# A list scheduler that keeps PSUM banks of the late attention reserved after their last reader

## The chip, the core and the metric

One core of a Trainium2 chip runs the whole program. The metric is device time in microseconds (us), median of the runs. The engines are TensorE (PE; its weight loads are listed as PEld), VectorE (DVE), ScalarE (ACT), GpSimd (POOL) and SyncE (SP), which issues most DMAs. Each engine takes its own instructions in the order in which they were written, and an instruction that waits holds up all behind it on that engine.

## What is computed

Windowed attention over 4 batch elements of 8 heads, 576 rows and 64 columns, and behind it two MLPs over the 2304 resulting rows of 512. Cut to what matters:

```python
scores = scale * np.matmul(q, k.transpose(0, 1, 3, 2))
masks = np.stack([mask_plain if h < H // 2 else mask_dil for h in range(H)], axis=0)
scores = np.where(masks[None, :, :, :], scores, -1000000000.0)
scores = scores - np.max(scores, axis=-1, keepdims=True)
attn = np.exp(scores)
attn = attn / (np.sum(attn, axis=-1, keepdims=True) + 1e-09)
x = np.matmul(attn, v)          # as (2304, 512) rows
h = x @ w_in1;  x = np.maximum(0.01 * h, h) @ w_out1
h = x @ w_in2;  out = (np.maximum(h, 0.0) + np.log1p(np.exp(-np.abs(h)))) @ w_out2
```

The arrays are float64 in the reference; the kernel converts the weights from their 8-byte form on the chip, and carries every product operand as two parts (a high and a low one), so that each logical product is three matmuls.

## The kernel before

**Stages.** The first MLP works on blocks of rows (`BLOCKS`: 256, 256, 352, then five of 288). For each block it walks 16 slices of the hidden layer: `g1` (line 715, 12 matmuls into bank `h`), an activation and a split on ACT (lines 731, 736) and DVE (line 740, `gl`), and two slots later `g2` (line 758, 12 matmuls into the four banks `yp`). The second MLP (`g3`, again line 715, and `g4`, line 854) begins after all blocks. Attention is cut into 8 windows of 288 rows with 4 pairs of heads each; window 0 and 1 are computed ahead of the first block ("early"), the windows 2 to 7 ("late") beside the MLP blocks before them: a window's result is the input of the block of the same number, so its last pair must be done when that block opens. I write "pair 6.3" for window 6, pair 3 (pairs 0 and 1 have the plain mask, 2 and 3 the dilated one).

**One late pair** is a chain over four engines: `trans_k`, `trans_q` (DVE, lines 510 and 517) - `scores` half 0 and half 1 (PE, line 562, each into a PSUM bank of tag `at`) - `mask` half 0 and 1 (DVE, line 576: adds the mask, PSUM bank to SBUF tile `s`) - `rowmax` (POOL, line 586) - `less_max` (DVE, line 590) - `exp` (ACT, line 593) - `pv_late` (PE, line 642, into an `at` bank) beside `sums` (POOL, line 650) - `spread` (DVE, line 658, needs both) - `recip` (DVE, lines 663 to 666) - `norm` (DVE, line 670, reads the `pv` bank) - `x_hi` (ACT, line 689) - `x_lo` (DVE, line 693, tile `xl`). There are only two `at` banks, one buffer `mx` for the two reductions of POOL (freed by `less_max`, then by `spread`) and two buffers of `s`.

**The same DVE** converts the weights: per piece a shift (268), a join (272), an add (281) and a split (311, tile `w`). The pieces of the first MLP are converted between the start and about 152 us, just ahead of their first use; those of the second are converted later, between the other work, and stored to DRAM.

**What sets the order.** No engine's order is written by hand. Each step is an `Op` with an engine, an assumed cost, `deps` (data), `acq` and `rel` (buffers it takes and frees) and a priority worked out backwards from due times. `run_schedule` walks time forward: when an engine is free it takes the ready operation of the least priority value whose buffers are free, and appends it to the result; the program is then emitted in that order. So the costs and delays in `Op` only set the order: on the chip, an instruction goes as soon as its engine, its inputs and its buffer are there. Three rules of the planner matter here. A buffer in `rel` is counted free the moment its reader ends:

```python
                _, _, o = heapq.heappop(finish)
                for r in o.rel:
                    free[r] += 1
```

An operation counts as ready a small delay (`lag`) after its inputs; PE operations of the late attention get `SLACK` on top (1.0 us before):

```python
            return late.get(a.eng, LATS if a.eng == b.eng else LAT) + b.slack
    ...
    NSPIN, LOCK, SLACK0, SLACK = 150, 1.2, 0.3, 1.0
```

And DVE operations marked `lock=True` are put back while a POOL reduction has just begun (`LOCK`, `WAIT`), since POOL and DVE get into each other's way there.

## Time and profile before

| | |
|---|---|
| median of 3 runs | 947.0 us (946.5 to 950.6) |
| the profiled execution | 947.08 us, of which the trace's span is 945.2 us |
| PE busy / weight loads | 907.5 us (96%) / 847.6 us (90%) |
| DVE busy | 728.5 us (77%) |
| ACT busy, POOL busy | 467.9 us (49%), 167.7 us (18%) |
| PE's granted clock, mean | 0.987 of full |

PE works nearly all the time, so what counts are the gaps that are left on it and the stretches at less than the full clock. The share of DVE hides that it is full in the stage in which the weights are converted and has room behind it. Up to about 60 us the early windows run; from 60 to about 475 us the first MLP with the late windows; behind that the rest of the first MLP and the second one, without attention.

### The profile page before, as it was taken

The numbers are of one execution on the slowest core, as the hardware profiler recorded it, in microseconds if no ns is written. First come the engines' busy times: TensorE is split into PE (matmuls) and PEld (weight loads), VectorE is DVE, ScalarE is ACT, GpSimd is POOL, SyncE is SP. The second block draws the span as 40 slices with busy tenths as digits, with TensorE's granted clock in tenths as the row PEclk, the third lists the DMA queues.
The fourth block names the chain that finished last, engine by engine and source line by source line (L and its number), as shares of the span: only waits on it lengthen the run. The fifth ranks groups of instructions, "written<-read, shape, count | busy, mean of one in ns | idle before, by whom it ended". The sixth has DMA issues, their size and how long they took to land.

```text
span 945.2 us, 15673 instructions
## 1 busy us (share of the span) xinstructions
PE 907.5 (96%) x5963; PEld 847.6 (90%) x5964; DVE 728.5 (77%) x1312; ACT 467.9 (49%) x935; POOL 167.7 (18%) x81
## 2 busy tenths in 40 slices
PE   6899988999999999899999999999999999999998
PEld 4789978999999999799999989989999899899996
DVE  3999998299696995977956787877877877877775
ACT  3768743334344353344447754544644645544544
POOL 5501233053251452423600000000000000000000
PEclk9979989999999999999999999999999999999999
DMA  8787113244445444433148700200200000000000
GB/s 225 213 245 254 20 27 54 70 116 128 126 109 140 102 126 121 123 106 124 54 152 266 243 27 1 68 1 1 68 1 1 34 1 0 34 1 1 34 1 34
DMA packets 139903, 81.51 MB, mean 86 GB/s; under 512 B 101172, under 2 KB 124724, under 8 KB 139828
## 3 DMA queue, kind: packets, MB, share of 16 engines
q1 hardware_dynamic: 137428, 79.92, 29.5%
q8 instruction: 47, 0.77, 0.3%
q10 hardware_dynamic: 2400, 0.59, 0.3%
q14 instruction: 28, 0.23, 0.1%
HBM read 62.65 MB, written 17.83 MB: 85 GB/s over the span
## 4 chain that ended last, share of the span: by engine, by line
PE 47%; DMA 1%; DVE 1%; ACT 1%; issue 0%; SPq 0%; DVEq 0%
PE h L715 23%; PE yo L854 21%; PE yp L758 3%; DMA raw<-in_moe_w_in_dram 1%; DMA w<-w 0%; DVE cf L272 0%; DMA y<-ys 0%; ACT hc L812 0%; ACT hc L811 0%; ACT w L308 0%; ACT ln L814 0%; DVE gl L841 0%; ACT gh L837 0%; DVE gl L740 0%; DVE cf L281 0%
## 5 line engine op out<-in xcount | busy, mean ns | idle before, releaser
L715 PE MATMUL h<-xh,w 128*128 128x384 f32 (+3 forms) x1792 | 446.2, 318 | 2.4 <-DVE w L311 2.2
L715 PEld LDWEIGHTS h<-xh,w 128*128 128x128 f32 x1792 | 315.4, 190 | 8.3 <-DVE w L311 3.3
L715 PE MATMUL h<-xl,w 128*128 128x384 f32 (+3 forms) x896 | 282.5, 315 | 0.3 <-DVE xl L693 0.3
L758 PE MATMUL yp<-gh,w 128*128 128x288 f32 (+2 forms) x1024 | 230.2, 300 | 0.7 <-DVE ys L768 0.7
L854 PE MATMUL yo<-w,gh 128*128 128x512 f32 x576 | 180.4, 394 | 1.4 <-ACT gh L837 1.4
L715 PEld LDWEIGHTS h<-xl,w 128*128 128x128 f32 x896 | 170.6, 190 | 4.8 <-DVE xl L693 0.5
L758 PEld LDWEIGHTS yp<-gh,w 128*128 128x128 f32 x1024 | 172.6, 189 | 1.8 <-DVE ys L768 1.0
L758 PE MATMUL yp<-gl,w 128*128 128x288 f32 (+2 forms) x512 | 151.7, 296 | 2.7 <-DVE gl L740 2.6
L811 ACT ACTIVATE hc<-h 128x384 f32<-128x384 f32 x96 | 47.1, 490 | 180.4 <-PE h L715 180.4
L854 PEld LDWEIGHTS yo<-w,gh 128*128 128x128 f32 x576 | 106.9, 188 | 19.6 <-ACT gh L837 2.6
L731 ACT ACTIVATE hc<-h 128x288 f32<-128x288 f32 (+2 forms) x128 | 52.0, 406 | 132.0 <-PE h L715 126.2
L854 PE MATMUL yo<-w,gl 128*128 128x512 f32 x288 | 114.4, 397 | 0.7 <-DVE gl L841 0.7
L650 POOL PARTITION_ALL_REDUCE sm<-s x24 | 92.8, 3866 | 59.7 <-ACT s L593 59.7
L740 DVE TENSOR_TENSOR gl<-hc,gh 128x288 fp32r<-128x288 f32 (+2 forms) x128 | 78.6, 616 | 31.9 <-ACT gh L736 31.0
L758 PEld LDWEIGHTS yp<-gl,w 128*128 128x128 f32 x512 | 96.9, 189 | 3.2 <-DVE gl L740 3.1
L822 DVE TENSOR_SCALAR z<-hc 128x384 f32<-128x384 f32 x96 | 34.5, 359 | 75.7 <-ACT hc L812 75.6
L586 POOL PARTITION_ALL_REDUCE mx<-s x24 | 49.5, 2061 | 224.1 <-DVE s L576 209.9
L854 PEld LDWEIGHTS yo<-w,gl 128*128 128x128 f32 x288 | 54.1, 188 | 14.1 <-DVE gl L841 1.7
L281 DVE CUSTOM_DVE_ANT_0 cf<-raw,cf 128x1024 uint16<-128x1024 uint16 (+1 forms) x48 | 62.2, 1295 | 1.5
L263 ACT ACTIVATE cf<-raw 128x512 f32<-128x512 f32 (+1 forms) x48 | 39.9, 831 | 42.4 <-DMA raw<-in_moe_w_in_dram 17.9
L736 ACT ACTIVATE gh<-hc 128x288 fp32r<-128x288 f32 (+2 forms) x128 | 56.7, 443 | 3.3
L841 DVE TENSOR_TENSOR gl<-ln,gh 128x384 fp32r<-128x384 f32 x96 | 53.5, 558 | 3.3 <-ACT gh L837 1.4
(83 smaller groups left out, 1040.2 us busy)
## 6 DMA issues: line engine op xcount, KB each, us to landing
raw<-in_moe_w_in_dram SPq DMA_DIRECT2D x32, 512.0 KB
raw<-in_moe_w_out_dram SPq DMA_DIRECT2D x32, 512.0 KB
w<-cf SPq DMA_DIRECT2D x32, 256.0 KB
w<-w SPq DMA_DIRECT2D x32, 256.0 KB
out_dram<-o SPq DMA_DIRECT2D x18, 256.0 KB
qr<-in_q_dram SPq DMA_DIRECT2D x96, 36.0 KB
y<-ys SPq DMA_DIRECT2D x20, 144.0 KB
v<-in_v_dram SPq DMA_DIRECT2D x30, 64.0 KB
```

The lines of the kernel that those rows point to most:

```text
L263: nc.scalar.activation(out=self.cff, in_=self.raw[:, :, 1].bitcast(F32), func=AF.Copy, scale=2.0 ** -112)
L281: nc.vector.tensor_tensor(out=self.cf, in0=self.cf, in1=self.raw[:, :, 0], op=ALU.add)
L586: nc.gpsimd.partition_all_reduce(self.mx, self.sf, channels=P, reduce_op=bass_isa.ReduceOp.max)
L650: nc.gpsimd.partition_all_reduce(self.sm, self.sf, channels=P, reduce_op=bass_isa.ReduceOp.add)
L715: nc.tensor.matmul(out=h, lhsT=a[:, c, :], rhs=b_[:, c, :], start=(c == 0 and a is whi and b_ is xh), stop=(c == NC - 1 and a is wlo))
L731: nc.scalar.activation(out=hc, in_=hbank.pop(s), func=AF.Prelu, alpha=0.01)
L736: nc.scalar.activation(out=gh, in_=hcopy[s], func=AF.Copy)
L740: eng.tensor_sub(out=gl, in0=hcopy.pop(s), in1=gparts[s][0].bitcast(F32))
L758: nc.tensor.matmul(out=ybank[e][:, o:o + n], lhsT=a[:, e * P:(e + 1) * P], rhs=b_, start=(f == 0 and n == unit_len[u] and a is whi and b_ ...
L811: nc.scalar.activation(out=ex, in_=hbank[NS1 + s], func=AF.Abs)
L841: nc.vector.tensor_sub(out=gl, in0=soft.pop(s)[1], in1=gparts[NS1 + s][0].bitcast(F32))
L854: nc.tensor.matmul(out=obank[c, t], lhsT=a[:, t * P:(t + 1) * P], rhs=b_, start=(f == 0 and a is gh and b_ is whi), stop=(f == NF - 1 and ...
```

## The change

The operations get a number `hold`: when the planner ends an operation with a hold, the buffers in its `rel` come free that much later in the plan. `mask` (both halves) and `norm` of the late windows get `HOLDS` = 1.5, so that each of the two `at` banks is counted as taken for 1.5 us more. `SLACK` goes from 1.0 to 2.0: `scores` and `pv_late` of the late windows count as ready 1 us later. And `x_lo` of the late windows is marked `lock`. No instruction is added, removed or altered; only the order on each engine moves.

```diff
+            self.skip, self.hold = False, hold
...
+            while held and held[0][0] <= now + 1e-9:
+                for r in heapq.heappop(held)[2].rel:
+                    free[r] += 1
             while finish and finish[0][0] <= now + 1e-9:
                 _, _, o = heapq.heappop(finish)
-                for r in o.rel:
-                    free[r] += 1
+                if o.hold:
+                    heapq.heappush(held, (o.end + o.hold, o.n, o))
+                    heapq.heappush(events, o.end + o.hold)
+                else:
+                    for r in o.rel:
+                        free[r] += 1
...
-    NSPIN, LOCK, SLACK0, SLACK = 150, 1.2, 0.3, 1.0
+    NSPIN, LOCK, SLACK0, SLACK, HOLDS = 150, 1.2, 0.3, 2.0, 1.5
...
-                cs = [Op("dve", dve(4 * a.m, True), a.mask, 0, deps=[s0], rel=["at"], **m)]
+                cs = [Op("dve", dve(4 * a.m, True), a.mask, 0, deps=[s0], rel=["at"], hold=HOLDS, **m)]
...
-                cs.append(Op("dve", dve(2 * (a.nt - 2) * a.m, True), a.mask, 1, deps=[a.o_s1], rel=["at"], **m))
+                cs.append(Op("dve", dve(2 * (a.nt - 2) * a.m, True), a.mask, 1, deps=[a.o_s1], rel=["at"], hold=HOLDS, **m))
...
-                xt = Op("dve", dve(288, True), a.norm, deps=[t], rel=["at"], **m)
+                xt = Op("dve", dve(288, True), a.norm, deps=[t], rel=["at"], hold=HOLDS, **m)
...
-            xl = Op("dve", dve(288, early), a.x_lo, deps=[xh], rel=[a.room(p)[1] if early else "xn"],
+            xl = Op("dve", dve(288, early), a.x_lo, deps=[xh], rel=[a.room(p)[1] if early else "xn"], lock=not early,
```

Lines of the changed file lie up to 7 higher. Three places show what that does to the order. The first is PE where the second half of the scores of pair 6.3 stands (`sc` is the `at` bank of scores, `pv` that of `pv_late`, `yp` a bank of `g2`, `h` one of `g1`). Before:

```order
L758 MATMUL yp_4512<-gl,w 128x288
L758 MATMUL yp_4512<-gh,w 128x288
L642 MATMUL pv<-s,v_94 64x72 x8
L562 MATMUL sc<-qz_91,kt_93 128x144 x2
L715 MATMUL h<-xh,w 128x288
L715 MATMUL h<-xl,w 128x288
```

Half 0 of the pair stands twelve matmuls of `g2` and `pv` of pair 6.2 ahead of this; half 1 is the third of three `at` writers in a row. After:

```order
L722 MATMUL h<-xl,w 128x288
L722 MATMUL h<-xh,w 128x288
L569 MATMUL sc<-qz_91,kt_93 128x144 x4
L765 MATMUL yp_4493<-gh,w 128x288
L765 MATMUL yp_4493<-gl,w 128x288
```

Both halves now stand side by side, ahead of `g2`, of one `g1` and of `pv` of pair 6.2. The second place is DVE from `less_max` of pair 6.1 to its `norm`. Before:

```order
L590 TENSOR_TENSOR s<-s,mx 128x576
L268 TENSOR_SCALAR cp<-cf 128x512
L740 TENSOR_TENSOR gl<-hc,gh 128x288
L272 SCALAR_TENSOR_TENSOR cf<-cf,cp 128x512
L281 ISA cf<-raw,cf 128x1024
L658 STREAM_TRANSPOSE xn<-sm 64x288 x2
L576 TENSOR_TENSOR s<-sc,masks 128x288
L663 TENSOR_SCALAR rd<-xn 128x9
L665 RECIPROCAL rd<-rd 128x9
L666 STREAM_TRANSPOSE xn<-rd 128x288
L740 TENSOR_TENSOR gl<-hc,gh 128x288
L670 TENSOR_TENSOR xn<-pv,xn 128x288
```

The mask of pair 6.2's first half stands behind `spread` (`xn<-sm`), which waits for POOL. After:

```order
L597 TENSOR_TENSOR s<-s,mx 128x576
L583 TENSOR_TENSOR s<-sc,masks 128x288
L747 TENSOR_TENSOR gl<-hc,gh 128x288
L288 ISA cf<-raw,cf 128x1024
L583 TENSOR_TENSOR s<-sc,masks 128x288
L747 TENSOR_TENSOR gl<-hc,gh 128x288
L524 STREAM_TRANSPOSE qz_90<-qr 64x288 x2
L517 STREAM_TRANSPOSE kt_92<-kr 128x320
L665 STREAM_TRANSPOSE xn<-sm 64x288 x2
L670 TENSOR_SCALAR rd<-xn 128x9
L672 RECIPROCAL rd<-rd 128x9
L673 STREAM_TRANSPOSE xn<-rd 128x288
```

Both masks of pair 6.2 now stand ahead of the `spread` of pair 6.1. The third place is DVE at the split of the last weight piece of the first MLP (line 311 before, 318 after). Before:

```order
L281 ISA cf<-raw,cf 128x2048
L663 TENSOR_SCALAR rd<-xn 128x9
L665 RECIPROCAL rd<-rd 128x9
L666 STREAM_TRANSPOSE xn<-rd 128x288
L740 TENSOR_TENSOR gl<-hc,gh 128x256
L670 TENSOR_TENSOR xn<-pv,xn 128x288
L590 TENSOR_TENSOR s<-s,mx 128x576
L311 TENSOR_TENSOR w<-cf,w 128x2x512
L693 TENSOR_TENSOR xl<-xn,xh 128x288
```

After:

```order
L288 ISA cf<-raw,cf 128x2048
L665 STREAM_TRANSPOSE xn<-sm 64x288 x2
L747 TENSOR_TENSOR gl<-hc,gh 128x256
L670 TENSOR_SCALAR rd<-xn 128x9
L672 RECIPROCAL rd<-rd 128x9
L673 STREAM_TRANSPOSE xn<-rd 128x288
L318 TENSOR_TENSOR w<-cf,w 128x2x512
L677 TENSOR_TENSOR xn<-pv,xn 128x288
L597 TENSOR_TENSOR s<-s,mx 128x576
L700 TENSOR_TENSOR xl<-xn,xh 128x288
```

`norm` of pair 2.2 and `less_max` of pair 2.3 now stand behind that split, and one more `gl` stands ahead of it; over everything ahead of that split, these three are the only instructions that changed sides.

## Rows read from the trace of the kernel before

**Rows 1.** The page's first line: the span of the trace.

```profile
span 945.2 us, 15673 instructions
```

**Rows 2.** Busy time of the engines by stage, us from the span's start.

```profile
core 0: us, PE busy (x) PEld busy (x) DVE busy (x) ACT busy (x) POOL busy (x), PEclk, DMA share, GB/s
60.00:100.00 40.00, 40.00 (x345) 39.74 (x345) 39.32 (x52) 30.21 (x48) 7.22 (x2) 1.00 0.74 246
100.00:150.00 50.00, 44.20 (x344) 42.35 (x341) 48.51 (x70) 28.00 (x44) 15.24 (x5) 0.90 0.16 29
...
470.00:945.00 475.00, 469.29 (x2512) 428.10 (x2510) 350.18 (x683) 243.77 (x504) 3.14 (x1) 1.00 0.15 48
```

**Rows 3.** Waits of PE, whole span: us in total, times, longest.

```profile
PE sc L562 <- DVE s L576: 7.1, 7, 2.2
...
PE sc L562 <- DVE xn L670: 0.8, 1, 0.8
```

**Rows 4.** Timeline of pair 4.2's scores, and a later add: start, length, engine, line.

```profile
264.00 3.93 POOL L650 PARTITION_ALL_REDUCE sm<-s  x1 [2.16 <-ACT s L593]
...
264.51 2.91 DVE L281 CUSTOM_DVE_ANT_0 cf<-raw,cf 128x1024 uint16<-128x1024 uint16 x1
267.97 0.96 DVE L658 STREAM_TRANSPOSE xn<-sm 64x288 f32<-64x288 f32 x2 [0.55 <-POOL sm L650]
268.95 0.46 DVE L576 TENSOR_TENSOR s<-sc,masks 128x288 f32<-128x288 f32 x1
...
269.47 0.76 PE L562 MATMUL sc<-qz,kt 128*128 128x144 f32 x4 [1.38 <-DVE s L576]
...
288.07 0.68 DVE L281 CUSTOM_DVE_ANT_0 cf<-raw,cf 128x1024 uint16<-128x1024 uint16 x1
```

**Rows 5.** Timeline around the second half of the scores of pair 6.3.

```profile
397.47 2.99 DVE L281 CUSTOM_DVE_ANT_0 cf<-raw,cf 128x1024 uint16<-128x1024 uint16 x1
400.38 0.45 DVE L576 TENSOR_TENSOR s<-sc,masks 128x288 f32<-128x288 f32 x1
...
400.88 1.32 PE L562 MATMUL sc<-qz,kt 128*128 128x144 f32 x4 [2.21 <-DVE s L576]
```

**Rows 6.** PE alone by stretch: length, busy (count), granted clock, DMA share, GB/s.

```profile
400.00:405.00 5.00, 4.12 (x21) 0.66 0.78 238
```

**Rows 7.** DVE's timeline up to the split of the last weight piece.

```profile
123.02 2.75 DVE L740 TENSOR_TENSOR gl<-hc,gh 128x256 fp32r<-128x256 f32 x1
...
149.44 0.38 DVE L740 TENSOR_TENSOR gl<-hc,gh 128x256 fp32r<-128x256 f32 x1
149.75 0.45 DVE L670 TENSOR_TENSOR xn<-pv,xn 128x288 f32<-128x288 f32 x1
150.12 0.74 DVE L590 TENSOR_TENSOR s<-s,mx 128x576 f32<-128x576 f32 x1
150.78 1.22 DVE L311 TENSOR_TENSOR w<-cf,w 128x1024 fp32r<-128x1024 f32 x1
```

**Rows 8.** PE's waits from 150 to 160 us: total, times, longest.

```profile
PE h L715 <- DVE w L311: 1.3, 1, 1.3
```

**Rows 9.** Timeline at the opening of block 3: DVE, then PE.

```profile
233.93 0.68 DVE L693 TENSOR_TENSOR xl<-xn,xh 128x288 fp32r<-128x288 f32 x1 [0.22 <-ACT xh L689]
...
234.67 0.40 PE L715 MATMUL h<-xl,w 128*128 128x288 f32 x1 [0.26 <-DVE xl L693]
```

**Rows 10.** Timeline of window 5: pair 5.1 on POOL and PE, then block 5.

```profile
325.22 4.07 POOL L650 PARTITION_ALL_REDUCE sm<-s  x1 [2.40 <-ACT s L593]
...
326.55 0.72 PE L642 MATMUL pv<-s,v 128*64 128x96 f32 x12
...
352.96 0.69 DVE L693 TENSOR_TENSOR xl<-xn,xh 128x288 fp32r<-128x288 f32 x1
...
356.24 0.29 PE L715 MATMUL h<-xl,w 128*128 128x288 f32 x1
```

**Rows 11.** Chain that ended last, 484 to 488 us: start, length, what.

```profile
485.84 1.60 PE yp L758 x12
```

More of the change, by code (lines that the diff above doesn't have):

```diff
@@ L91, in __init__ @@
         def __init__(self, eng, cost, fn, *args, deps=(), order=(), acq=(), rel=(),
-                     target=None, margin=0.0, start=0.0, lib=None, slack=0.0, lock=False, optional=False):
+                     target=None, margin=0.0, start=0.0, lib=None, slack=0.0, lock=False, optional=False, hold=0.0):
             self.eng, self.cost, self.fn, self.args = eng, cost, fn, args
@@ L99, in __init__ @@
             self.lib, self.slack, self.lock, self.optional = lib, slack, lock, optional
-            self.skip = False
+            self.skip, self.hold = False, hold
             self.n = len(ops)
@@ L160, in run_schedule @@
         filled = []
-        finish = []
+        finish, held = [], []
         while True:
             moved = False
+            while held and held[0][0] <= now + 1e-9:
+                for r in heapq.heappop(held)[2].rel:
+                    free[r] += 1
             while finish and finish[0][0] <= now + 1e-9:
                 _, _, o = heapq.heappop(finish)
-                for r in o.rel:
-                    free[r] += 1
+                if o.hold:
[4 more added lines that the diff above has]
+                        free[r] += 1
                 for u in o.users:
```

## The prediction

> **What bounds the kernel now.** I read the page first, then the busy times by stage, then PE's waits, then the timeline at each wait. The page gives a span of 945.2 us [rows 1]; the execution took 947.08 us, so 1.9 us lie around the span, and the median of the runs, 947.0 us, is the same number. The sum below is made against 947.1. The last 475 us hold no attention and PE is busy 469.3 of them [rows 2]: this change moves nothing there, it can only let that stretch begin sooner or later. So the question is how many gaps of PE lie between 60 and 470 us, and which of them the new order touches.
>
> There are two kinds of stage. From 60 to 150 us DVE is busy 39.3 of 40 and 48.5 of 50 us [rows 2]: it converts the weights, and PE waits for it. There a better place for PE's instructions is worth nothing by itself; only what DVE does ahead of the last weight piece counts, since PE stands waiting for that piece at 152 us (1.3 us, [rows 8]). From 152 us on PE is the bound and each gap on it is paid in full. In that part nearly all of PE's waiting is one kind: `scores` waiting for `mask`, 7.1 us in 7 waits, the longest 2.2, and once for `norm`, 0.8 us [rows 3]. A `scores` instruction needs nothing new from its own pair's mask; it waits because the mask's bank is the one it is to write.
>
> Why the masks are late is seen at two of the seven. At pair 4.2 the reduction `sums` runs on POOL from 264.00 for 3.93 us; a DVE add that starts half a microsecond later takes 2.91 us, where the same add at 288 us takes 0.68; `spread` waits for POOL and starts at 267.97; the mask stands behind it at 268.95, and PE has idled 1.38 us when it starts at 269.47 [rows 4]. At pair 6.3 the same add takes 2.99 us, the mask behind it starts at 400.38, and PE has idled 2.21 us [rows 5]. So each time POOL reduces, DVE loses some 2 us that the planner does not know of, while PE's next bank writer was planned right behind the mask. [...]
>
> **The change part by part.**
>
> *Banks held 1.5 us longer and `scores` ready 1 us later, windows 4 to 7.* The order shows what comes of it. For pairs .2 and .3 both halves of `scores` stand side by side or one `g1` apart, ahead of the previous pair's `pv`, and both masks of pair .2 stand ahead of the `spread` of pair .1, so they no longer wait for POOL. For pairs .1 the second half stands one `g2` further behind the mask that it waits for. A `g2` of 12 matmuls lasts 1.60 us [rows 11]. That is more than the wait of 1.38 [rows 4], and twice what the six others than the longest come to on average ((7.1 - 2.2) / 6 = 0.8, [rows 3]). The wait of 2.21 us [rows 5] goes because its mask stood behind a held add, and half 1 of that pair now needs no mask of its own first half; its bank is now that of `norm` of pair .1, which stands behind `spread`, `recip` and a few others. So I take the whole 7.1 us off and put 0.5 us back for `scores` that now wait for such a `norm`: the one such wait before was 0.8 [rows 3], the pairs concerned are four, so the bounds of that item are 0 and 3.2 us, and the order leaves a `g1` and half a `g2` more room than there was at the 0.8, so I stay near the lower end. Term: -6.6, bounds -7.1 and -3.9.
>
> *The clock.* The stretch of 400 to 405 us ran at 0.66 [rows 6], that is (1 - 0.66) x 5 = 1.7 us of lost work of PE at the higher level. It follows the longest wait. If the waits go, so does this. Term: -1.7, bounds -1.7 and 0 (another gap could call it).
>
> *The weight stage, window 2.* What stands ahead of the last split changed by three DVE instructions: `less_max` 0.74 and `norm` 0.45 behind it, one `gl` of 0.38 ahead of it [rows 7], net -0.8 us. The split ends at 152.0 and PE waits for it [rows 8], so this goes through to PE. Unknown is which DVE instructions start in a POOL reduction now: before, one `gl` took 2.75 in place of 0.38 us [rows 7]; the order of POOL is the same. One such hold more or less is 2.4 us. Term: -0.8, bounds -3.2 and +1.6. The idle time and the lower clock (0.90 from 100 to 150, [rows 2]) of PE in this stage give nothing back, as long as the split is what PE waits for.
>
> *Window 3.* The wait for `norm` of 0.8 us goes [rows 3]; but PE reaches block 3 sooner, where it already waits 0.26 us for `x_lo` of pair 3.3 [rows 9], and that `x_lo` comes no sooner: it ends a chain of POOL reductions. The scores of pair 4.0, moved ahead of that place, are PE work that fills a part of it. Term: 0, bounds -0.8 and +1.3: one DVE hold of 2.4 us [rows 7] less the moved scores, six matmuls, of which four of a like size last 0.76 [rows 4], so 1.1 by estimate from that row.
>
> *`x_lo` marked `lock`.* It moves that instruction by a place or two among DVE's own. It has a margin: in window 5, `xl` of the last pair ends at 353.65 and is first read at 356.24, 2.6 us later [rows 10]. Term: 0 as long as the margin holds; without that cover each block's opening pays.
>
> *Queues.* POOL's order does not change at all; on SP and ACT a few DMA issues and splits trade places with neighbours, and no wait of PE in these stages is for either. Term: 0.
>
> Sum: 947.1 - 6.6 - 1.7 - 0.8 + 0 = **938.0 us**.
>
> [...]
>
> **The rivals.**
>
> *The chain comes late, the blocks wait.* Holding banks delays the scores and `pv` in the order, the chain of a window gets longer, and the time that PE saves is handed back where the next block opens: PE comes there about 2 us sooner per window ((6.6 + 1.7) / 4), and the margin was 2.6 us [rows 10]. If the chain also comes 2.6 us later, all of the 8.3 is given back: 947.1 - 0.8 = 946.3. For it: `pv` is one `g2` and up to two halves of scores later. Against it: `spread` needs `pv` and `sums`, and `pv` of pair 5.1 ended at 327.27 while `sums` ended at 329.29 [rows 10], 2.0 us later, so a `pv` 1.6 us later is still hidden by POOL; and the masks ahead of `spread` let the next `rowmax` start sooner. [...]
>
> *Slower: `pv` overtaken.* The same place, one step on. If `pv` ends after `sums` by d, each of a window's four pairs is d later, since one buffer `mx` makes them follow one another; the last `x_lo` comes 4d late, and with a margin of 2.6 us every opening of blocks 3 to 7 pays 4d - 2.6. It decides from d = 0.65. At d = 1, that is `pv` moved by 3.0 in place of 1.6 to 2.4 us, the five openings cost 7 us, and the saved waits are lost too: 946.3 + 7 = 953. Against it: the room of 2.0 us and that PE itself has fewer gaps ahead of `pv`.
>
> *Another hold ahead of the last split.* One DVE instruction more caught in a reduction between 60 and 150 us: +2.4, and PE's shortfall grows with it; the rest as forecast: 940.4, or 942 with two fallen badly. Faster still, but less.
>
> *The change does not do what it says* is out for the places shown: the order has moved there.
>
> **How the numbers follow.** A measurement of this kernel can tell about 0.5% (4.7 us) from no change, so "faster" begins below 942.3 and "slower" above 951.7. Forecast and extra hold together 0.70 (0.58 and 0.12), of which 0.66 lie below 942.3; the chain that hands the gain back 0.19 (942 to 947); the overtaken `pv` 0.11 (951.7 and up, most of it). Faster 0.66, same 0.22, slower 0.12. The range: the best bounds together give 947.1 - 7.1 - 1.7 - 3.2 - 0.8 = 934.3; at the upper end the rival at 946.3 is cut a little short: 934 to 945.5.
>
> **What would show it.** After: PE's waits for `mask` near 0 in windows 4 to 7 (7.1 before), waits of `scores` for `norm` under 2 us in all, no stretch under full clock after 160 us, the last split of the first MLP between 149 and 154 us, PE's waits for `xl` at the five openings under 1 us in all, and the stage without attention as long as before. It would be wrong if the waits turn up under another name in the same places (`xl`, `norm`, `gl`), or if the weight stage ends later than 154 us.

## The result, and the profile after

The changed kernel takes 938.3 us (median of 4 runs, 935.5 to 940.3) against 948.2 us for the kernel before in the same comparison: ratio 0.9891, 95% interval 0.9855 to 0.9928, faster by about 1.1%. A second comparison gave 937.5 us and 0.9901 (0.9876 to 0.9925). The forecast was 938.0 in a range of 934.0 to 945.5. The profiled execution took 935.5 us with a span of 933.6, that is 11.6 us less than the span in [rows 1], where the sum had 9.1; the medians are 9.9 us apart, since the profiled execution is the fastest of the four.

PE's waits after, whole span (us in total, times, longest), answering [rows 3]; the lines of the code are 7 further down than before, so `scores` is L569, `mask` L583, `norm` L677, `y_evac` L775, `x_lo` L700:

```profile
PE sc L569 <- DVE xn L677: 4.1, 3, 2.1
PE h L722 <- DVE w L318: 3.9, 4, 1.8
...
PE yp L765 <- DVE ys L775: 2.3, 3, 1.3
```

and two rows of the same view before:

```profile
PE h L715 <- DVE w L311: 2.2, 3, 1.3
...
PE yp L758 <- DVE ys L768: 0.7, 1, 0.7
```

The line `sc <- DVE s`, 7.1 us before, is not there at all. Three other lines grew: `scores` behind a `norm` (0.8 before, 4.1 now), `g1` behind a weight split (2.2 before, 3.9 now, all of it in the stage in which PE waits for the weights anyway) and `yp` behind the evacuation of a `y` bank (0.7 before, 2.3 now). From 235 to 475 us, which is blocks 3 to 6 and the opening of block 7, only the `ys` waits and this row are left; the other two `norm` waits, 2.1 and 1.8 us, stand at 136 and 233 us:

```profile
PE sc L569 <- DVE xn L677: 0.2, 1, 0.2
```

PE alone by stretch after (length, busy, granted clock, DMA share, GB/s); the third row answers [rows 6]:

```profile
135.00:140.00 5.00, 2.71 (x13) 0.78 0.34 53
140.00:145.00 5.00, 5.00 (x27) 0.54 0.00 0
400.00:405.00 5.00, 5.00 (x42) 1.00 0.55 100
235.00:470.00 235.00, 232.51 (x1851) 1.00 0.43 117
```

and the last of these stretches in the kernel before:

```profile
235.00:470.00 235.00, 226.81 (x1778) 0.99 0.42 114
```

PE is busy 5.7 us more of the 235, and the granted clock is full throughout (1.00). How the same DVE hold looks now, at pair 6.3 (timeline: start, length, engine, line), answering [rows 5]:

```profile
391.70 1.14 PE L569 MATMUL sc<-qz,kt 128*128 128x144 f32 x8
393.35 3.71 POOL L657 PARTITION_ALL_REDUCE sm<-s  x1 [1.85 <-ACT s L600]
393.52 0.45 DVE L583 TENSOR_TENSOR s<-sc,masks 128x288 f32<-128x288 f32 x1
393.89 2.67 DVE L288 CUSTOM_DVE_ANT_0 cf<-raw,cf 128x1024 uint16<-128x1024 uint16 x1
396.46 0.46 DVE L583 TENSOR_TENSOR s<-sc,masks 128x288 f32<-128x288 f32 x1
```

The add is still held (2.67 us in place of 0.68) and the second mask still stands behind it, some 2 us late. But both halves of the scores were issued before, in one row of eight matmuls at 391.70, so nothing on PE waits for that mask. DVE instructions of over 2.3 us between 235 and 470 us number 9 before and 11 after: the holds did not become fewer, they stand where nobody waits.

Where the 11.6 us of span came from is read by comparing marks in the two traces: the end of the last weight split of the first MLP, the end of ACT's first `hc` instruction of each block (L731 before, L738 after), of the last one, and of the trace. Each row is the difference to the kernel before, in us (negative is earlier); the kernels from the third row on are those of the experiments. Each row rests on one profile, and the kernel before has only one, while its own runs lay between 943.4 and 952.8 us in one comparison of 23; so a difference of 2 us in a single mark is not the edit's work unless a wait or a stretch below the full clock explains it:

```
                    split  blk 2  blk 3  blk 4  blk 5  blk 6  blk 7   last    end
changed             -2.27  -2.37  -0.34  -2.04  -2.57  -7.68 -10.27  -9.89 -11.59
changed, again      -1.91  -2.01  -0.85  -2.49  -2.97  -8.17 -10.75  -8.31  -8.69
holds only          -1.88  -1.92  -1.31  -2.24  -2.26  -7.11  -9.44  -8.64 -10.83
readiness only      -1.37  -1.38  -0.42  -3.20  -2.53  -7.96  -5.20  -5.89  -6.54
pair 4.0 late       -2.94  -2.97  -0.64  -2.68  -3.23  -6.37  -8.61  -9.42  -6.59
window 3 short      -4.81  -3.35  -3.47  -5.13  -5.66 -10.92 -13.51 -11.53 -12.93
holds 3.0           -5.50  -5.49  +0.50  +3.42  +7.51  +5.00  +8.28  +9.72  +6.39
readiness 1.4       -1.66  -0.26  -0.97  -1.20  -0.03  -1.96  -4.19  -4.10  -3.33
readiness 1.7       -1.88  +0.74  +1.88  +8.02  +7.62  +4.31  +2.02  +0.69  +1.63
no reservation      -2.69  -2.75  -0.35  -2.12  -2.68  -7.08  -9.84  -8.25  -9.55
reservation only    +1.06  +1.04  +1.08  +1.73  +2.11  +3.54  +2.66  +2.08  +5.43
six writes for sums -6.39  -4.93  -6.57  -8.00  -8.82 -13.51 -14.59 -15.92 -13.42
one write for sums  -7.24  -7.25  -8.89 -11.69 -12.69 -18.17 -19.52 -20.40 -19.80
```

For the changed kernel: 2.4 us are gained up to block 2, 2.0 of them are lost again in window 3 (between the marks of blocks 2 and 3), 9.6 are gained from block 3 to the last block, and 1.7 after it, in the stage without attention.

### The profile page after: what moved, and what is told of

It reads as the page before. It is cut to its first block, busy times and chain, and to the rows that moved or that the text cites. A ratio compares the mean times of both kernels' runs of the same rounds, so it can differ in the third digit from the quotient of the medians.

```text
span 933.6 us, 15670 instructions
## 1 busy us (share of the span) xinstructions
PE 902.4 (97%) x5963; PEld 844.0 (90%) x5964; DVE 723.4 (77%) x1312; ACT 464.6 (50%) x935; POOL 168.7 (18%) x81
## 4 chain that ended last, share of the span: by engine, by line
PE 83%; DVE 6%; DMA 5%; issue 1%; SPq 1%; ACT 1%; DVEq 0%; ACTq 0%
PE h L722 40%; PE yo L861 21%; PE yp L765 18%; PE sc L569 2%; DMA raw<-in_moe_w_out_dram 2%; PE pv L649 1%; DMA w<-w 1%; DVE w L318 1%; DMA y<-ys 1%; SPq L462 1%; DVE cf L279 1%; DVE cf L288 1%; DMA raw<-in_moe_w_in_dram 0%; DVE qz L524 0%; DVE rd L670 0%
## 5 line engine op out<-in xcount | busy, mean ns | idle before, releaser
L738 ACT ACTIVATE hc<-h 128x288 f32<-128x288 f32 (+2 forms) x128 | 51.7, 404 | 114.7 <-PE h L722 114.5
L288 DVE CUSTOM_DVE_ANT_0 cf<-raw,cf 128x1024 uint16<-128x1024 uint16 (+1 forms) x48 | 55.0, 1145 | 1.7 <-ACT raw L284 0.3
```

Source lines behind the costliest of these rows:

```text
L288: nc.vector.tensor_tensor(out=self.cf, in0=self.cf, in1=self.raw[:, :, 0], op=ALU.add)
L738: nc.scalar.activation(out=hc, in_=hbank.pop(s), func=AF.Prelu, alpha=0.01)
```

## The experiments

**The theory**: a DVE instruction that runs beside a POOL reduction is held (2.91 us in place of 0.68 in [rows 4]), a mask behind it is late, and PE stands because its next bank writer was put right behind that mask; the change helps by putting room there. **The rivals**: PSUM is too small and the gaps only move; or the gain comes from the weight stage and the clock.

### What makes the mask late: two kernels with the reduction taken out

Both start from the kernel before, in its order.

```diff
-            nc.gpsimd.partition_all_reduce(
-                self.sm, self.sf, channels=P, reduce_op=bass_isa.ReduceOp.add)
+            for _ in range(6):
+                nc.gpsimd.memset(self.sm, 1.0)
```

> The kernel before in its order. In windows 2 to 7 the reduction of the softmax sums across partitions on GpSimd is left out (so the division there has the wrong denominators), and six plain writes of the same tile stand in its place: GpSimd is busy for a similar time (3.6 to 4.2 us before), but reads nothing. It tells apart what makes the mask late. Theory (a DVE instruction that runs beside the reduction is held by it): the DVE instructions of 2.7 to 3.9 us beside the late sums fall to their usual 0.4 to 1.3 us, the waits of PE for mask of the kind at 397.47 (add held, mask behind it) go; those that come from spread waiting for GpSimd's end stay: 1.5 to 4 of the 7.1 us are left. Rival (GpSimd's length alone, by spread ahead of the mask in DVE's order): the 7.1 us stay, whatever GpSimd does in that time. Rival (a plain write holds DVE just as long): held DVE instructions as before, 7.1 us stay.

```diff
-            nc.gpsimd.partition_all_reduce(
-                self.sm, self.sf, channels=P, reduce_op=bass_isa.ReduceOp.add)
+            nc.gpsimd.memset(self.sm, 1.0)
```

> As the kernel with six writes, but one write only: in windows 2 to 7 the reduction of the softmax sums is left out, and GpSimd is done in about a sixth of the time. Theory (either way in which GpSimd makes the mask late): mask waits of PE in windows 4 to 7 under 1 us in all, and the span 5 to 10 us shorter than before; 937 to 942 us. Rival (masks are late for another reason, PSUM or DVE's own load): 4 us or more of mask waits stay.

Timeline of the kernel with six writes, pair 6.2; the first row is POOL, about as long as the reduction was:

```profile
385.24 3.93 POOL L651 MEMSET sm<- 128x576 f32 x6 [0.98 <-DVE s L590]
...
387.59 0.69 DVE L281 CUSTOM_DVE_ANT_0 cf<-raw,cf 128x1024 uint16<-128x1024 uint16 x1
388.20 0.45 DVE L576 TENSOR_TENSOR s<-sc,masks 128x288 f32<-128x288 f32 x1
```

PE's waits of that kernel, 235 to 475 us, first row:

```profile
PE sc L562 <- DVE s L576: 1.7, 4, 0.7
```

The add beside the writes takes 0.69 us, as it does alone. Of 19 such adds beside writes none takes over 0.71, and no DVE instruction from 235 to 470 us takes over 2.3 us (9 before). So the reduction held DVE here, and writes of the same total length did not. The mask waits fall from 7.1 to 1.7 us, the span of the profiled run by 13.4; the median of only two runs is 936.3 us, ratio 0.9890 (0.9838 to 0.9941).

It would be wrong to conclude that the 5.4 us that went were the holds. What the late masks of the kernel before waited for stands in its own trace. Six of the seven masks stand right behind a `spread`, and DVE idles ahead of that `spread` until `sums` ends: at pair 4.2 in [rows 4] (0.55 us), and at the five others here:

```profile
256.56 0.96 DVE L658 STREAM_TRANSPOSE xn<-sm 64x288 f32<-64x288 f32 x2 [0.79 <-POOL sm L650]
...
317.54 0.96 DVE L658 STREAM_TRANSPOSE xn<-sm 64x288 f32<-64x288 f32 x2 [0.18 <-POOL sm L650]
...
377.50 0.96 DVE L658 STREAM_TRANSPOSE xn<-sm 64x288 f32<-64x288 f32 x2 [0.78 <-POOL sm L650]
...
388.89 0.96 DVE L658 STREAM_TRANSPOSE xn<-sm 64x288 f32<-64x288 f32 x2 [0.55 <-POOL sm L650]
...
442.87 0.96 DVE L658 STREAM_TRANSPOSE xn<-sm 64x288 f32<-64x288 f32 x2 [0.18 <-POOL sm L650]
```

The held instruction was over by then (nine adds of 2.9 to 3.0 us from 160 to 475 us all end 0.52 us before their reduction), so without the hold DVE would only have idled longer. These six waits of PE (0.64, 1.38, 0.35, 0.78, 1.37 and 0.39) are 4.9 of the 7.1 us: they come from POOL's length. Only the seventh, the 2.21 us of [rows 5], has a held add and no `spread` ahead of its mask. The six writes took most of the 4.9 us away by ending sooner: they do not need `exp`, so they start right behind `less_max`. At pair 6.1 the stand-in ends 4.8 us after `less_max` began, the reduction 5.5, and PE's wait there falls by as much, from 1.37 to 0.65. All four waits that are left stand behind a `spread` that waits for POOL, as here:

```profile
378.76 0.96 DVE L658 STREAM_TRANSPOSE xn<-sm 64x288 f32<-64x288 f32 x2 [2.04 <-POOL sm L651]
```

With one write (POOL done in 0.6 us) none of PE's waits stands behind such a `spread` any more, 0.5 us of mask waits is left, and the time is 927.3 us (two runs). That kernel came out 10 us below the lower end of what I had put; 8.9 of its 19.8 us are there at block 3 already, since the reductions of windows 2 and 3 go too. So both ways lead back to the reduction: 4.9 us by its length, 2.2 by what it holds. The plan knows neither: it counts `sums` at 2.2 us, and the late ones take 3.6 to 4.2. A plan with the measured length, the obvious other remedy, was not run.

Which DVE instructions are held shows in the kernel before as well. Beside late `sums` the add (two inputs in SBUF) takes 1.86 us on average against 0.68 alone (17 and 10 instructions; nine of the 17 are held, at 2.9 to 3.0 us, and the other eight, most of which begin just before the reduction or near its end, take their usual time); the mask, which reads one input from PSUM, takes 0.45 beside and 0.45 alone (10 and 30). Beside the writes, which read no tile, the same add takes 0.69 us in the kernel with six of them. What on the chip makes these differences no run here shows. So the mask itself is not slow; it is late because of what stands ahead of it.

### One part of the change at a time

```diff
-    NSPIN, LOCK, SLACK0, SLACK, HOLDS = 150, 1.2, 0.3, 2.0, 1.5
+    NSPIN, LOCK, SLACK0, SLACK, HOLDS = 150, 1.2, 0.3, 1.0, 1.5
...
-            xl = Op(... rel=[a.room(p)[1] if early else "xn"], lock=not early,
+            xl = Op(... rel=[a.room(p)[1] if early else "xn"],
```

> The holds of 1.5 alone: the longer reading of PE's readiness goes back from 2.0 to 1.0, and the reservation around x_lo is taken out. In the order, the scores of pair 4.0 stay behind the opening of block 3, as in the kernel before; the second halves of scores stand one g2 further from the mask they need. Theory (a held DVE makes a mask late; room in PE's order hides that): mask waits of PE in windows 4 to 7 under 1 us in all (7.1 before, 0 after), no wait of 1.8 us of pair 4.0 for norm and no waits of block 3 for ys, so window 3 does not give back its 3.0 us; 936 to 941 us. Rival A (PSUM is too small, the gaps only move): the waits come back under xl, norm or gl at the openings, 944 to 947. Rival B (the gain of the changed kernel comes from the weight stage and the clock, not from the banks): mask waits fall, but the span falls by under 3 us unless the last weight split ends near 150 us.

935.9 us, ratio 0.9881 (0.9848 to 0.9915): the time of the changed kernel. No mask wait, no `norm` wait, no `ys` wait from 175 us on. In their place stands this row (waits of PE, 175 to 475 us):

```profile
PE pv L649 <- ACT s L600: 4.1, 4, 1.3
```

that is, with the shorter readiness `pv` stands too near behind its `exp`, once in each of windows 3 to 6.

```diff
-    NSPIN, LOCK, SLACK0, SLACK, HOLDS = 150, 1.2, 0.3, 2.0, 1.5
+    NSPIN, LOCK, SLACK0, SLACK, HOLDS = 150, 1.2, 0.3, 2.0, 0.0
```

(and `lock` taken out as above)

> The longer readiness (2.0 in place of 1.0) alone, no holds, no reservation around x_lo. In the order the pairs .2 and .3 of a window have room behind their masks, but the second half of scores of the pairs .1 still stands right behind its mask. Theory: about half of the 7.1 us of mask waits stays (three or four waits of 0.35 to 2.2 us, at the pairs .1 of windows 4 to 7), the rest is gone; 940 to 944 us. Rival A (PSUM too small): as before or worse, 945 to 948. Rival B (weight stage and clock): mask waits do not matter, the time goes with the end of the last weight split: 938 if that is near 150 us, 944 or more if it is near 152.

940.3 us, ratio 0.9937 (0.9897 to 0.9978; the interval overlaps that of the changed kernel), the time I expected, but not for the reason: I had read from the order that half of the mask waits would stay, and none did. Either half of the change is enough to remove all of them. What its profile lacks against the changed kernel's is one event:

```profile
424.05 0.46 DVE L775 COPY ys<-yp 128x288 f32<-128x288 f32 x1 [3.63 <-DMA y<-ys]
...
424.56 0.40 PE L765 MATMUL yp<-gh,w 128*128 128x288 f32 x1 [3.36 <-DVE ys L775]
```

```profile
425.00:430.00 5.00, 5.00 (x27) 0.67 0.71 239
```

A `y` bank's evacuation waits 3.63 us for the store of an earlier `ys` buffer, PE stands 3.36 us, and the granted clock of the next 5 us is 0.67: 3.4 + 0.33 x 5 = 5.0 us. In the table its lead over the changed kernel at block 6 (0.3 us) turns into 5.1 us behind at block 7. That one wait accounts for the difference of the two spans (5.1 us).

```diff
-    NSPIN, LOCK, SLACK0, SLACK, HOLDS = 150, 1.2, 0.3, 2.0, 1.5
+    NSPIN, LOCK, SLACK0, SLACK, HOLDS = 150, 1.2, 0.3, 1.0, 0.0
```

> The third part alone: the reservation of DVE ahead of x_lo of the late windows, no holds, readiness 1.0 as before. The order of PE differs from the kernel before in four places. Theory: mask waits of PE stay near 7 us in windows 4 to 7, and the time is that of the kernel before, 945 to 949. Rival (the chain's last x_lo sets the openings, and the reservation is what helps): xl at the openings earlier, 940 to 943.

951.1 us, ratio 1.0025 (0.9996 to 1.0053), the mask waits at 7.6 us in 8 waits. The reservation alone does nothing that can be measured.

The rival of the weight stage is not ruled out by these times: the split ends at 150.1 us with the holds only (935.9 us) and at 150.6 with the readiness only (940.3 us), and that rival allowed such gains for a split near 150. It is ruled out by the marks. At block 3 the changed kernel, the holds only and the readiness only lead by 0.3, 1.3 and 0.4 us; from there to the last block they gain 9.6, 7.3 and 5.5, where the weight stage is over. Nor is it the clock: the one stretch below full clock in that part, at 0.66, is worth 1.7 us at most [rows 6]. And with the same banks the mask waits go from 7.1 us to 0 by order alone, and all of PE's waits from 235 to 475 us from 8.3 to 2.5, so PSUM was not too small for this.

### Where window 3 lost 2 us

My first reading was pair 4.0: its scores moved some 15 us earlier (from 245.3 to 230.1), ahead of block 3, waited for a `norm`, and its `sums` held an add ahead of `y_evac`. From the changed kernel's timeline:

```profile
232.17 0.45 DVE L677 TENSOR_TENSOR xn<-pv,xn 128x288 f32<-128x288 f32 x1
...
232.68 0.59 PE L569 MATMUL sc<-qz,kt 128*128 128x192 f32 x2 [1.80 <-DVE xn L677]
...
238.86 3.70 POOL L657 PARTITION_ALL_REDUCE sm<-s  x1 [1.74 <-ACT s L600]
239.37 2.67 DVE L288 CUSTOM_DVE_ANT_0 cf<-raw,cf 128x1024 uint16<-128x1024 uint16 x1 [0.26 <-ACT raw L284]
...
244.29 0.53 DVE L775 COPY ys<-yp 128x352 f32<-128x352 f32 x1 [1.82 <-DMA y<-ys]
...
244.87 0.40 PE L765 MATMUL yp<-gh,w 128*128 128x288 f32 x1 [1.28 <-DVE ys L775]
```

So I kept that pair's scores behind the opening of block 3 and left all else as it was:

```diff
-                        order=[prev(1, "o_s1")], **ms)
+                        order=[prev(1, "o_s1")], start=232.0 if (w, p) == (4, 0) else 0.0, **ms)
```

> The changed kernel, with the scores of one pair (4.0) kept behind the opening of block 3 by an earliest time of their own. Theory for the 3.0 us that window 3 lost (pair 4.0 came 13 us earlier, waited 1.80 us for norm of pair 3.3, and its sums held a DVE add of 2.67 us ahead of y_evac, for which PE then waited 0.22 and 1.28 us): the ys waits near 243 to 245 us and the norm wait near 232 us are gone, the opening of block 3 stays bound by x_lo of pair 3.3, the mask waits stay at 0; 1.5 to 2.5 us below the changed kernel, 934 to 937. Rival A (window 3 is bound by the chain of its own pairs whatever pair 4.0 does): the waits turn up as xl at the opening of block 3, same time as the changed kernel, 937 to 939. Rival B (pair 4.0 late makes the chain of window 4 late): xl or norm waits of 2 us or more at block 4, 939 to 941.

That missed: 941.3 us, ratio 0.9931 (0.9908 to 0.9954), not faster than the changed kernel but some 3 us slower (the two intervals just overlap). The waits for `norm` and `ys` are gone from 230 to 245 us, and at the opening of block 3 stands this instead:

```profile
231.94 0.45 DVE L677 TENSOR_TENSOR xn<-pv,xn 128x288 f32<-128x288 f32 x1
232.43 0.69 ACT L696 ACTIVATE xh<-xn 128x288 fp32r<-128x288 f32 x1 [1.94 <-DVE xn L677]
...
233.17 0.40 PE L722 MATMUL h<-xh,w 128*128 128x288 f32 x1 [1.95 <-ACT xh L696]
```

The `norm` of pair 3.3 starts at 231.9 here, 232.2 in the changed kernel, and 232.7 before; the split ends at 149.1, 149.7 and 152.0. PE waits for that `norm` under whichever name comes first. The loss is what rival A of that run says, the chain of window 3's own pairs; the name was `xh` and not `xl`, and the time lies above the 937 to 939 us that it gave. What else this kernel lost, 4.5 us from the last block to the end against the changed kernel, lies at the entry of the stage without attention (last section).

The chain itself was then shortened in window 3 only, in the changed kernel's order:

```diff
+            if self.w == 3:
+                nc.gpsimd.memset(self.sm, 1.0)
+            else:
                 nc.gpsimd.partition_all_reduce(
                     self.sm, self.sf, channels=P, reduce_op=bass_isa.ReduceOp.add)
```

> The changed kernel; in window 3 alone the reduction of the softmax sums on GpSimd is left out and one write of the same tile stands in its place (the division there has the wrong denominators). Theory (block 3 opens when the chain of window 3's four pairs ends, near 234 us, whatever PE saved before; the weight stage's 2.3 us are given back there): with the chain shorter, no wait of scores for norm near 232 us, no held DVE instruction in the chain, and the lead of 2.4 us of block 2 is kept at the first hidden-layer step of block 3; the span is 2 to 4 us below the changed kernel. Rival (window 3 lost its time to pair 4.0's early place, its norm wait and its sums, which hold DVE ahead of y_evac; those sums stay): the lead at block 3 is regained at the opening, but 1.5 us go again to the ys waits near 242 to 245 us: under 1.5 us below the changed kernel. Rival 2 (PE itself is full in window 3): same time as the changed kernel.

> The changed kernel itself, for a comparison with the three next ones on the same chip. 936 to 940 us; mask waits 0, block 3 opens 0 to 0.6 us earlier than in the kernel before although the last weight split ends 2.3 us earlier.

933.6 us against 937.5 for the changed kernel on the same chip. The same place in its timeline:

```profile
229.04 0.45 DVE L680 TENSOR_TENSOR xn<-pv,xn 128x288 f32<-128x288 f32 x1
...
229.54 0.59 PE L569 MATMUL sc<-qz,kt 128*128 128x192 f32 x2 [0.22 <-DVE xn L680]
```

The `norm` comes 3.1 us earlier, and of its lead at block 2 nothing is given back at block 3 (-3.35 and -3.47 in the table; the changed kernel -2.37 and -0.34, and -2.01 and -0.85 in its second profile). So the chain is the cause of the waiting: whatever PE and DVE save ahead of 232 us in this kernel is kept only as far as the chain of window 3 lets it. PE alone between the marks of blocks 2 and 3, before, changed and with window 3 short, shows that not all of the 2.0 us is waiting:

```profile
166.66:235.66 69.00, 67.97 (x468) 1.00 0.40 106
164.29:235.32 71.03, 68.73 (x474) 1.00 0.41 106
163.31:232.19 68.88, 68.66 (x474) 1.00 0.42 110
```

PE stands idle 1.0, 2.3 and 0.2 us. The other 0.8 us of the 2.0 is work: the six matmuls of pair 4.0's scores, which the next stretch then no longer has. The `ys` waits near 240 us stay at 0.24 and 1.29 us, as that run's rival said; they cost, but they are not the 2 us. Of the 4.2 us between the two spans on this chip, about 1.3 were there at block 2 already, which this edit can't have caused: the first reduction that it replaces starts at 187.75 us, and its last split ended at 147.2, where the same DVE order gave 149.1, 149.7 and 150.1 in the other profiles. With such a spread, 2.9 us, one profile says little about the weight stage.

### More of the same: longer holds, and readiness in between

```diff
-    NSPIN, LOCK, SLACK0, SLACK, HOLDS = 150, 1.2, 0.3, 2.0, 1.5
+    NSPIN, LOCK, SLACK0, SLACK, HOLDS = 150, 1.2, 0.3, 2.0, 3.0
```

> The changed kernel with the holds doubled, 3.0 in place of 1.5. Mask waits of PE are 0 already with 1.5. Theory: nothing is left to gain behind the masks; the scores of a pair go further from the tiles they follow, and the cost is in the chain: 936 to 942 us, not faster than the changed kernel by more than 1 us. Rival A (more room, more gain): under 935. Rival B (holding banks longer makes the chain late, xl and norm waits of more than 3 us in all at blocks 4 to 7): 942 to 950.

953.4 us, ratio 1.0071 (1.0045 to 1.0096): slower than the kernel before, with no mask wait at all. The theory of that run missed; its rival B named the cause and put the time too low. Its waits have this in first place (whole span):

```profile
PE h L722 <- ACT xh L696: 13.0, 5, 4.6
```

Five openings, blocks 3 to 7, each waits for its window's chain: 4.62, 2.49, 1.97, 1.47 and 2.46 us. Around them the granted clock is 0.74, 0.57, 0.66, 0.70 and 0.96 in the rows of 5 us that begin at 230, 235, 300, 425 and 430 us, which is (0.26 + 0.43 + 0.34 + 0.30 + 0.04) x 5 = 6.9 us; about 0.9 of them cost nothing, since PE stood until 234.18 us, in the first of these rows. 13.0 + 6.0 less the 3.1 us by which it was ahead of the changed kernel at block 2 is 15.9 of the 18.0 us between the spans. That counts the large items only: the changed kernel has its own 1.8 us of waiting ahead of block 3, and this one has 3.0 us of `pv` waiting for `exp` besides. This is the prediction's rival of the chain that comes late, at a place where it decides.

The changed kernel with readiness 1.4 and 1.7 in place of 2.0, both without the reservation, was meant to take the `pv` waits out of the kernel with the holds only:

> Holds of 1.5 as in the changed kernel, readiness 1.4 in place of 2.0, no reservation around x_lo. With the holds alone (readiness 1.0) PE waited 0.9 to 1.3 us for exp ahead of pv once in each of windows 3 to 6, 4.1 us in all; with readiness 2.0 it did not, but ys and norm waits stood there. In the order pair 4.0 stays behind the opening of block 3. Theory (the room between exp and pv is what the holds alone lack): exp waits at about half, 1 to 2.5 us in all, mask waits under 0.5, 934 to 936 us. Rival (what is gained there is given back at the openings, which the chain binds, as with pair 4.0 kept late): 936 to 939, xl or xh waits of over 1.5 us.

> As the one with 1.4, with readiness 1.7. In the order the room between exp and pv is about as long as in the changed kernel. Theory: exp waits gone (4.1 us with the holds alone), mask waits under 0.5, pair 4.0 behind the opening of block 3: 932 to 936 us. Rival (given back at the openings): 936 to 941, xh waits of 0.4 us or more at the openings of blocks 3 to 7.

Both missed, theory and rival. 947.3 us, ratio 1.0002 (0.9976 to 1.0028) with 1.4, and 949.7 us, 1.0028 (1.0009 to 1.0048) with 1.7. With 1.4 the profiled run took 943.8 us, 3.5 below the median, so what its slower runs lost is not seen; in this one two mask waits came back (1.24 and 1.31 us), `pv` waits 1.5 us for `exp` and 1.8 for other ACT work. With 1.7 there is no mask wait and no `exp` wait, but:

```profile
244.88 5.52 SPq L778 DMA_DIRECT2D y<-ys  x4
...
249.53 0.52 DVE L775 COPY ys<-yp 128x352 f32<-128x352 f32 x1 [4.30 <-DMA y<-ys]
...
250.11 0.61 PE L765 MATMUL yp<-gh,w 128*128 128x288 f32 x1 [4.13 <-DVE ys L775]
```

```profile
245.00:250.00 5.00, 0.98 (x6) 0.85 0.49 164
250.00:255.00 5.00, 4.89 (x19) 0.50 0.48 141
```

SP takes 5.52 us to issue the stores of four `y` tiles; there are three `ys` buffers, so the fourth evacuation waits for an earlier store, and PE for it. What slows these stores is not shown; in the changed kernel SP issued three of them in 2.66 us, at 242.5. The row at 0.85 is nearly all waiting (PE busy 0.98 of 5 us), so the clock costs what the second row shows, 0.50 x 4.89 = 2.4 us. With the wait of 4.13 that is 6.6 us. Between block 3 and block 4 this kernel falls back by 6.1 us against the kernel before, which has 2.0 us of mask waits there itself; so this one event is most of the 8.1 us to be explained, and not all. Since these two kernels also lacked the reservation, one more run closed that gap:

```diff
-            xl = Op(... rel=[a.room(p)[1] if early else "xn"], lock=not early,
+            xl = Op(... rel=[a.room(p)[1] if early else "xn"],
```

> The changed kernel without its third part, the reservation of DVE ahead of x_lo (holds 1.5, readiness 2.0); the order of PE differs in two places, that of DVE in eight. It ends the series of kernels with holds 1.5 and no reservation, at readiness 1.0, 1.4 and 1.7 (935.9, 947.3 and 949.7 us). Theory (what counts is where single DVE instructions fall, and here the order is the changed kernel's): 936 to 940 us, mask waits 0. Rival (the reservation is what the kernels with 1.4 and 1.7 lacked): 944 us or more, with waits of over 1 us for ys or xh that the changed kernel does not have.

936.1 us, ratio 0.9862 (0.9800 to 0.9923), no mask wait. So the reservation is worth nothing here either, and with the holds at 1.5 and no reservation, readiness 1.0, 1.4, 1.7 and 2.0 give 935.9, 947.3, 949.7 and 936.1 us. Nothing in the two numbers themselves explains that; each value is another order, and what the trace with 1.7 shows is a single event. None of the kernels that compute everything is faster than the changed one beyond the intervals; the holds alone do as well with one part in place of three. A fourth `ys` buffer, meant against the `ys` waits, was not tried.

## Why the prediction came out right, point by point

**Bank holds and readiness, -6.6.** That room in the order takes the waits away was right and is shown: mask waits 7.1 to 0, `scores` for `norm` 0.2 us in windows 4 to 7. (Over the whole span the `norm` waits came to 4.1 us, above the 2 that the prediction gave as a sign; 3.9 of them lie ahead of block 3.) Why the masks are late was read wrongly in part. "Each time POOL reduces, DVE loses some 2 us" made the held add the common cause; in [rows 4] itself DVE idles 0.55 us behind that add until `sums` ends, and so it is at six of the seven waits, 4.9 of the 7.1 us. The term did not hang on it: masks placed ahead of `spread`, and room behind the others, help whatever made the mask late. One thing was missing: the `y` evacuations (2.3 us after, 0.7 before), which the term did not list. By waits alone the stretch gains 7.1 - 0.2 - 1.6 = 5.3; with the 1.7 of clock 7.0; by the marks it is 9.6 from block 3 to the last block. Of the other 2.5 us, 0.8 is the six matmuls of pair 4.0 that moved ahead of block 3; the rest, under 2 us, I leave open.

**The clock, -1.7.** The row of 400 to 405 us is at 1.00 after, and no row from 150 to 930 us is below it. The 1.7 counts what 0.66 lacks to the full clock, 1.00 as from 60 to 100 us [rows 2]; it is an upper bound, since PE was busy only 4.12 of those 5 us [rows 6]. That it follows the longest wait is supported, but not a law: of eleven waits of 1.9 us or more between 160 and 560 us in all these traces seven are followed by rows at 0.50 to 0.80, four are not, and in four places the clock fell behind shorter waits, of 0.95 to 1.72 us. The kernel with one write, with no wait of 1 us there, shows no such row.

**The weight stage, -0.8.** PE waits for DVE only from 100 us on; from 60 to 100 us it is busy 40.0 of 40 [rows 2], which the prediction passed over. Measured -2.3 (-1.9 in the second profile), inside the bounds of -3.2 and +1.6. Two kernels with the same DVE order up to there ended the split 2.9 and 4.8 us earlier, so a single profile fixes this term to some 3 us only. The order's part was as counted; besides, DVE waits 0.4 in place of 1.1 us from 100 us on. The last split now, answering [rows 7]:

```profile
148.55 1.18 DVE L318 TENSOR_TENSOR w<-cf,w 128x1024 fp32r<-128x1024 f32 x1
149.65 0.45 DVE L677 TENSOR_TENSOR xn<-pv,xn 128x288 f32<-128x288 f32 x1
```

**Window 3, 0.** This is the step that failed: 2.0 us were lost, over the bound of 1.3 (1.2 in the second profile, inside it). 1.3 of the 2.0 are waiting and 0.8 the moved scores. The row was there: PE already waited 0.26 us for `x_lo` at block 3's opening [rows 9], so the chain bound that place before, and the prediction says itself that this `x_lo` comes no sooner. It priced the place by one DVE hold and some moved scores, and did not carry the weight stage's gain through the opening, where by the same row it had to be given back. Weight stage and window 3 together are -0.3, where the sum had -0.8: the gain ahead of the opening was worth next to nothing.

**The reservation and the queues, 0.** Right for the reservation, by two runs. The queues were not all nothing: the stores of `y` stand in SP's queue, and 1.6 us of new waits are theirs.

**The stage without attention, 0.** It was 1.7 us shorter, but that cannot be put down to the change: its second profile gave 0.4 us, and over the other kernels the same stretch lies between 3.3 us shorter and 3.4 us longer than before (last two columns of the table).

**The rivals.** The chain that comes late was real, but not at holds of 1.5. In the changed kernel `pv` of pair 5.1 stands so:

```profile
323.22 3.59 POOL L657 PARTITION_ALL_REDUCE sm<-s  x1 [1.97 <-ACT s L600]
326.01 0.72 PE L649 MATMUL pv<-s,v 128*64 128x96 f32 x12
```

It ends at 326.73, `sums` at 326.81: the room of 2.0 us of [rows 10] is 0.1 us now, as the estimate of 1.6 to 2.4 us said. In windows 4 to 7 the worst `pv` ends 0.5 us behind its `sums`, pair 4.0 apart. So one pair came close to that rival's point of 0.65 us, which it needs at all four pairs of a window. Doubling the holds did bring the late chain with its price (953), though not by a `pv` that stands far behind `sums` in each pair (at most 0.7 us in windows 4 to 7).

So the time was right by a sum with faults of opposite sign: 2.0 us lost in window 3, against 1.5 us more in the weight stage and 3 us more past block 3 than counted. That the median came out within 0.3 us of the forecast is luck; the profiled span fell by 2.5 us more than the sum.

## What to carry to other kernels

When an engine waits again and again for a bank, look at what stands ahead of the releasing instruction on its engine before giving the bank more room: here the releaser itself never took over 0.56 us. Then ask what the instruction ahead of it waited for: six times of seven it idled until a reduction on GpSimd ended, and only once was it one that took four times its usual time beside that reduction (2.99 us [rows 5] in place of 0.68 [rows 4]). A slow neighbour is not the cause of a delay that another wait covers. Room in the order hides such waits (7.1 to 0 us), but only up to the slack of the next chain: check each opening at which the engine already waits, however little, for there every gain made earlier ends. And a scheduler's parameter has no smooth response: four values of one number gave 936, 947, 950 and 936 us, so judge the order that comes out, by its single waits, not the value.

## What the chip showed that was not expected

Two waits were dearer than their length: 3.36 us on PE were followed by 5 us at a granted clock of 0.67 and cost 5.0 us by estimate from those two numbers; 4.13 us were followed by 5 us at 0.50 and cost 6.6.

Two profiles of the same changed kernel differ by 2.9 us in span, and all of it arises past block 7 (there the slower one was still 0.5 us ahead). What can be seen is the entry of the stage without attention: PE's matmuls there wait 0.5 us for `gh` in one and 2.0 in the other, and only the other has rows below full clock at 530 to 540 us (0.92 and 0.74; 0.98 over 470 to 545 us, where the first has 1.00). In the kernel with pair 4.0 late that entry costs most:

```profile
534.77 0.73 PE L861 MATMUL yo<-w,gh 128*128 128x512 f32 x2 [1.72 <-ACT gh L844]
...
536.14 0.61 PE L861 MATMUL yo<-w,gl 128*128 128x512 f32 x1 [0.64 <-DVE gl L848]
```

```profile
535.00:540.00 5.00, 4.36 (x13) 0.66 0.39 131
```

Why the entry falls out one way or the other in the same kernel is not settled by these runs.
